# Reordering the swaps of x on the sync queue: block 0's ahead of block 2's loads, block 1's between the two loads of block 2

## Chip, core, metric

One core of one Trainium2 chip. The metric is the device time of one execution in microseconds (us). The kernel before takes 156.68 us (median of 3 runs, 156.55 to 157.26). Profiled spans are about 1.7 us shorter than the times, because the span runs from the first to the last instruction.

## The reference, cut to what matters

```python
g = sigmoid((x * gate_w).sum(-1, keepdims=True))        # x: 2048 x 448
q, k, v = split(x @ wqkv)                               # 16 heads of 28
phi_q = concat(softmax(q @ w_phi), softmax(-q @ w_phi)) # per head, phi_k likewise
o = (phi_q @ (phi_k^T v)) / (phi_q . sum(phi_k)) @ wo   # linear attention
b = gelu(x @ w1 + b1) @ w2 + b2
out = g * o + (1 - g) * b
```

The kernel works on x transposed (channels on partitions), in four blocks of 512 rows, numbered 0 to 3. 448 channels are seven chunks of 64. For much of the work PE runs two 64-row matmuls side by side, one on the upper and one on the lower half of the partitions, so each half needs all seven chunks of its own block of x. Half of these chunks lie on the wrong partitions, and copies inside SBUF, the "swaps", bring them across.

## The kernel before

Block 0 is turned by PE. Blocks 1 to 3 come by transposing DMAs, each as a wide one (384 channels) and a narrow one (the last 128). All of this and the swaps is issued from the sync queue (SP), in this order:

```python
def load_x(b):                                          # transposed load of block b
    blk = slice(b * 512, (b + 1) * 512)
    nc.sync.dma_start_transpose(xT[:, 0:3, blk], x[blk, 0:384])     # wide
    nc.sync.dma_start_transpose(xT[:, 3, blk], x[blk, 320:448])     # narrow
def swap_x(h):                                          # blocks 2h (even) and 2h+1 (odd)
    nc.sync.dma_start(xS[0:HP, :, h, :], xT[HP:P, :, ev])           # even
    nc.sync.dma_start(xS[HP:P, 0:3, h, :], xT[0:HP, 0:3, od])       # odd
...
load_wT(WkT, D); load_wT(WqT, 0); load_x(1)
... # weights are prepared; POOL copies the last chunk of block 1:
nc.gpsimd.dma_start(x1o, xT[HP:P, 3, 512:1024])
load_x(2)
swap_w(WqS, Wpq)        # query weights, two copies
swap_x(0)
load_x(3)
swap_w(WkS, Wpk)        # key weights
swap_x(1)
swap_w(WvS, WvG, 3)     # value weights
... # then w1, wo, w2
k_pair(0); k_pair(1); k_pair(2); k_pair(3); v_both()    # keys, values of blocks 0, 1
for g in range(4): q_pair(g, 0)                         # first use of swap_x(0)
for r in range(4): k_two(r); v_two(r); q_pair(r, 1)     # first use of swap_x(1), WvS
```

v_both uses x1o. After this part PE goes on with the feed-forward and the output without waiting.

The softmax here doesn't subtract the row's maximum and nothing guards it: scores larger than these inputs give would overflow.

## Time and profile before

| | before |
|---|---|
| time, median | 156.68 us |
| PE busy | 149.5 us, 97% of the span |
| PE's waits | 1.1 us at the start, 0.9 us for the odd swap of blocks 0 and 1 |
| odd swap of blocks 0 and 1: issue, landing | 16.40, 20.99 |
| odd swap of blocks 2 and 3: issue, landing | 22.71, 26.7 |

A DMA has two times: its issue, drawn on the queue SPq, and its landing, when the data are there. "x2" behind a line is a count. The lines of the profile are shown in the prediction.

### The profile page before, as it was taken

The page shows a single profiled execution, that of the slowest core. Times are in us where ns is not written, and L with a number is a line of the kernel's source. Part 1 is how long each engine was busy: PE and PEld are TensorE (multiplying, and loading weights), DVE is VectorE, ACT ScalarE, POOL GpSimd, SP SyncE. Part 2 cuts the span into 40 slices and gives each one's busy share as a digit, 9 for nine tenths or more (in the row PEclk, how much of TensorE's full clock was granted, in tenths as well). Part 3 has the DMA queues.
Part 4 walks back from the last instruction along what each step waited for, and adds up shares of the span by engine and source line. Part 5 has one row for each costly group of instructions (what it writes and reads, how often), then busy time and mean ns, then how long its engine had stood idle before and what let it go on. Part 6 is the DMA issues. An engine that isn't in the chain of part 4 may idle for free.

```text
span 154.7 us, 3189 instructions
## 1 busy us (share of the span) xinstructions
PE 149.5 (97%) x1302; PEld 81.2 (53%) x1302; DVE 83.1 (54%) x244; ACT 77.2 (50%) x93; POOL 34.1 (22%) x38
## 2 busy tenths in 40 slices
PE   7999979999999999999999999999999999999991
PEld 2775435555555854444444455555556555555561
DVE  3454989379892050000000059999977999977100
ACT  2569919999889626776767640111311111111121
POOL 7951596919876000000000000000000000000000
PEclk9999999999999999999999999999999999999999
DMA  4999999999993000000000001114332124338401
GB/s 150 229 232 154 209 233 254 221 222 215 218 356 130 4 0 4 0 0 4 0 0 0 4 0 34 34 38 96 92 96 64 40 64 92 82 82 39 121 31 30
DMA packets 28306, 14.98 MB, mean 97 GB/s; under 512 B 19938, under 2 KB 27876, under 8 KB 28292
## 3 DMA queue, kind: packets, MB, share of 16 engines
q1 hardware_dynamic: 27012, 14.00, 42.1%
q10 hardware_dynamic: 1152, 0.65, 1.5%
q0 software_dynamic: 128, 0.13, 0.7%
q8 instruction: 10, 0.16, 0.4%
q14 instruction: 4, 0.03, 0.1%
HBM read 6.11 MB, written 1.84 MB: 51 GB/s over the span
## 4 chain that ended last, share of the span: by engine, by line
PE 84%; SPq 9%; DMA 3%; issue 1%; DVE 0%; ACT 0%; ACTq 0%
PE hp L442 27%; PE y L501 27%; PE pq L320 8%; PE y L507 8%; PE nm L457 4%; PE v_ps L304 3%; PE pk L312 3%; DMA xS<-xT 3%; SPq L136 3%; PE acc L331 2%; SPq L132 2%; SPq L133 2%; SPq L384 1%; SPq L126 1%; SPq L141 0%
## 5 line engine op out<-in xcount | busy, mean ns | idle before, releaser
L501 PE MATMUL y<-w_sb,gel 128*128 128x448 bf16 (+2 forms) x238 | 45.2, 341 | 0.0
L442 PE MATMUL hp<-xT,w_sb 64*128 64x512 bf16 x196 | 42.3, 376 | 0.0
L442 PE MATMUL hp<-xS,w_sb 64*128 64x512 bf16 x196 | 41.9, 376 | 0.0
L447 ACT ACTIVATE gel<-hp,b1T 128x1024 bf16<-128x1024 f32 x28 | 30.8, 1110 | 13.0 <-PE hp L442 13.0
L510 ACT ACTIVATE res<-y,ungate 128x448 bf16<-128x448 f32 (+2 forms) x17 | 10.4, 611 | 50.3 <-PE y L507 50.2
L501 PEld LDWEIGHTS <-gel 128*128 128x128 bf16 x238 | 22.6, 98 | 19.6
L442 PEld LDWEIGHTS <-w_sb 64*128 64x128 bf16 x392 | 19.6, 94 | 22.5
L276 POOL TENSOR_TENSOR phik<-phik,rec 128x1792 bf16<-128x1792 bf16 (+1 forms) x8 | 24.9, 3126 | 9.8 <-DVE rec L273 9.8
L462 DVE COPY st<-nm 128x32 f32<-128x32 f32 x32 | 4.5, 184 | 35.5 <-PE nm L457 35.5
L478 DVE TENSOR_TENSOR tmp<-nm,al 128x448 bf16<-128x448 f32 x32 | 18.4, 617 | 0.0
L271 DVE TENSOR_REDUCE sums<-phik 128x64 f32<-128x1792 bf16 x8 | 16.0, 2000 | 2.8 <-ACT phik L264 2.8
L507 PE MATMUL y<-wo_sb,oT 128*128 128x448 bf16 (+2 forms) x68 | 14.7, 342 | 0.0
L320 PE MATMUL pq<-xT,Wpq 64*128 64x512 bf16 x56 | 13.0, 376 | 0.0
L320 PE MATMUL pq<-xS,WqS 64*128 64x512 bf16 x56 | 11.2, 376 | 0.9 <-DMA xS<-xT 0.9
L325 ACT ACTIVATE EqP<-pq 128x1024 bf16<-128x1024 f32 x8 | 8.4, 1051 | 5.1 <-PE pq L320 5.1
L193 DVE CAST vaug<-v_ps 128x896 bf16<-128x896 f32 x7 | 7.5, 1081 | 6.0 <-PE v_ps L304 3.3
L326 ACT ACTIVATE EqN<-pq 128x1024 bf16<-128x1024 f32 x8 | 8.4, 1055 | 0.0
L457 PE MATMUL nm<-KVbd,EqP 128*128 128x120 bf16 x64 | 8.3, 216 | 0.0
L457 PE MATMUL nm<-KVbd,EqN 128*128 128x120 bf16 x64 | 8.3, 216 | 0.0
L263 ACT ACTIVATE phik<-pk 128x896 bf16<-128x896 f32 x8 | 7.7, 961 | 0.3 <-PE pk L285 0.3
L507 PEld LDWEIGHTS <-oT 128*128 128x128 bf16 x68 | 6.0, 98 | 3.5
L264 ACT ACTIVATE phik<-pk 128x896 bf16<-128x896 f32 x8 | 7.8, 972 | 0.0
(99 smaller groups left out, 147.2 us busy)
## 6 DMA issues: line engine op xcount, KB each, us to landing
w_sb<-in_B_w_dram SPq DMA_DIRECT2D x4, 784.0 KB, 14.1
out_dram<-res SPq DMA_DIRECT2D x15, 112.0 KB, 1.9
w_sb<-in_B_w_dram SPq DMA_DIRECT2D x1, 1568.0 KB, 16.1
xS<-xT SPq DMA_DIRECT2D x2, 256.0 KB, 4.0
oT<-in_A_x_dram ACTq DMA_DIRECT2D x1, 448.0 KB, 3.2
xS<-xT SPq DMA_DIRECT2D x2, 192.0 KB, 4.3
WvS<-WvG SPq DMA_DIRECT2D x2, 168.4 KB, 3.9
wo_sb<-in_A_wo_dram SPq DMA_DIRECT2D x1, 336.0 KB, 17.1
```

What stands on the lines that cost most here:

```text
L271: nc.vector.reduce_sum(out=sums[:], in_=ph, axis=AX.X)
L276: eng.tensor_tensor(out=ph[:, lo:hi], in0=ph[:, lo:hi], in1=rec[:, lo:hi, :, None].to_broadcast([P, hi - lo, 2, DH]), op=ALU.mult)
L320: nc.tensor.matmul(pq[:, i, :], lhsT=w_half(Wpq, WqS, i, k)[:, g * P:(g + 1) * P], rhs=x_half(i, k, h), start=(k == 0), stop=(k == NK - 1))
L325: nc.scalar.activation(out=EqP[:, g, dst], in_=src, func=ACT.Exp)
L326: nc.scalar.activation(out=EqN[:, g, dst], in_=src, func=ACT.Exp, scale=-1.0)
L442: nc.tensor.matmul(hp[:, i, :], lhsT=w1_sb[i * HP:(i + 1) * HP, k, j * P:(j + 1) * P], rhs=x_half(i, k, h), start=(k == 0), stop=(k == NK ...
L447: nc.scalar.activation(out=gel[h][:, j, :], in_=hp[:].rearrange("p a b -> p (a b)"), func=ACT.Gelu_apprx_tanh, bias=b1T[:, j:j + 1])
L457: nc.tensor.matmul(nm[s][:, g * 2 * KW:(g + 1) * 2 * KW], lhsT=E[:, g, tok], rhs=KVbd[:, g, s, :], start=True, stop=True)
L478: nc.vector.tensor_tensor(out=tmp[:, s, :].rearrange("p (x h d) -> p x h d", x=NPR, h=2), in0=nmv[s][:, :, 0:PW].rearrange("p x (h d) -> p ...
L501: nc.tensor.matmul(y, lhsT=gel[t // 8][:, j, (t % 8) * P:(t % 8 + 1) * P], rhs=w2_sb[:, j, cols], start=(j == 0), stop=False)
L507: nc.tensor.matmul(y, lhsT=oT[:, c, tok], rhs=wo_sb[:, c, cols], start=False, stop=(c == NC4 - 1))
L510: nc.scalar.activation(out=res[:, cols], in_=y, func=ACT.Copy, scale=ungate[:, t:t + 1])
```

## The change

The intent: the odd swap is what PE waits for, so it is moved ahead of the narrow load of block 2, and the even swap, whose source is ready early, to the front.

```diff
-    load_x(2)
+    swap_x(0, "even")
+    load_x(2, "wide")
     swap_w(WqS, Wpq)
-    swap_x(0)
+    swap_x(0, "odd")
+    load_x(2, "rest")
     load_x(3)
```

load_x and swap_x get an argument that issues one of their two DMAs (cut here). Nothing else changes.

More of the change, by code (lines that the diff above doesn't have):

```diff
@@ L128, with load_x, swap_x @@
     nc.scalar.dma_start(wphi[:, 0:3, :], wphi_rows[0:384, :].rearrange("(c p) b -> p c b", p=P))
-    def load_x(b):
+    def load_x(b, part=None):
         blk = slice(b * 512, (b + 1) * 512)
-        nc.sync.dma_start_transpose(xT[:, 0:3, blk], x[blk, 0:384])
-        nc.sync.dma_start_transpose(xT[:, 3, blk], x[blk, 320:448])
+        if part != "rest":
+            nc.sync.dma_start_transpose(xT[:, 0:3, blk], x[blk, 0:384])
+        if part != "wide":
+            nc.sync.dma_start_transpose(xT[:, 3, blk], x[blk, 320:448])
     def load_wT(W, base):
         nc.sync.dma_start_transpose(W[:], A_wqkv[:, base:base + NC4 * P])
-    def swap_x(h):
+    def swap_x(h, part=None):
         ev = slice(2 * h * 512, 2 * h * 512 + 512)
         od = slice(2 * h * 512 + 512, 2 * h * 512 + 1024)
-        nc.sync.dma_start(xS[0:HP, :, h, :], xT[HP:P, :, ev])
-        nc.sync.dma_start(xS[HP:P, 0:3, h, :], xT[0:HP, 0:3, od])
+        if part != "odd":
+            nc.sync.dma_start(xS[0:HP, :, h, :], xT[HP:P, :, ev])
+        if part != "even":
+            nc.sync.dma_start(xS[HP:P, 0:3, h, :], xT[0:HP, 0:3, od])
     load_wT(WkT, D)
```

## The prediction

> **What bounds the kernel now.** I read the page first (busy shares and the chain that ended last), then PE's waits, then the timelines of PE and of the sync queue between 10 and 30 us, then the DMA's share in short windows. The page says that PE is the bound, and the list of PE's waits says how little of its time is not work:
>
> ```profile
> PE 149.5 (97%) x1302; PEld 81.2 (53%) x1302; DVE 83.1 (54%) x244; ACT 77.2 (50%) x93; POOL 34.1 (22%) x38
> PE 84%; SPq 9%; DMA 3%; issue 1%; DVE 0%; ACT 0%; ACTq 0%
> ...
> PE warm_ps L367 <- DVE w_sb L115: 1.1, 1, 1.1
> PE pq L320 <- DMA xS<-xT: 0.9, 1, 0.9
> ```
>
> The last two lines are all the waits of PE: 1.1 us at the very start, and one wait of 0.9 us, for a swapped copy of x. So the change can win at most this one hole. Behind it the chain is PE without a break to the end; ahead of it it is the sync queue, issuing DMAs one after the other:
>
> ```profile
> 10.27 1.71 SPq L132
> ...
> 12.03 1.26 SPq L133
> ...
> 13.47 0.56 SPq L383
> ...
> 14.08 1.52 SPq L384
> ...
> 16.40 4.59 DMA xS<-xT
> ```
>
> Columns are start, length, what. L132 and L133 are the wide and the narrow transposed load of x block 2, L383 and L384 the two swaps of the query weights; left out after them is L141, the even swap of x (source: block 0, issued at 15.64), and the last line is the odd swap (source: block 1), which lands at 16.40 + 4.59 = 20.99 us. PE's timeline shows what it holds up:
>
> ```profile
> 19.77 0.38 PE L320 MATMUL pq<-xT,Wpq 64*128 64x512 bf16 x1
> 21.03 0.39 PE L320 MATMUL pq<-xS,WqS 64*128 64x512 bf16 x2 [0.89 <-DMA xS<-xT]
> 21.24 0.39 PE L320 MATMUL pq<-xT,Wpq 64*128 64x512 bf16 x2
> ```
>
> The second matmul of the first query product (k = 0, lower half) is already one on the odd swap. Pairs start 0.21 us apart (21.03, 21.24), so without a wait it would have started at 19.77 + 0.21 = 19.98; it started at 21.03. The hole as it counts for the end is 21.03 - 19.98 = 1.05 us; the 0.89 is smaller because the matmul before is drawn to its modelled end.
>
> **What the skill says.** (1) The Trainium skill, "DMA: Bandwidth & Descriptors", section "Queues, rings and completion order": on each DMA engine descriptors are taken in ring order. The trace agrees as far as it goes: the copies that I could follow land in the order of issue (key swaps issued at 20.57 and 21.20 land 3.3 and 3.5 us later, the odd swap of blocks 2 and 3 from 22.71 after 4.0, the last value swap from 24.27 after 3.9). So moving an issue ahead of a transfer takes that transfer's time out of the landing. (2) "Perfetto Trace Analysis", section "DMA Instruction — HWDGE (DVE, Sync)": the issue's window is descriptor generation, not the data's movement. It agrees: 0.60 us of issue against 4.59 to landing. (3) "DMA: Bandwidth & Descriptors", section "Two DMAs through the same engine are not ordered": a copy that reads what an earlier DMA wrote has to wait for its completion. The odd swap reads block 1, loaded by DMA; the even one reads block 0, which came by PE transposes and DVE and ACT copies that end at 7.1 us. Neither wait binds: block 1's wide load, issued at 7.12, has 5.7 us to landing or less, so it is there by 12.8. (4) The same page, "Issuing engines are not separate DMA queues": the copy that POOL issues at 13.59 (x1o) shares the engines. The trace shows the collision below.
>
> **The change part by part.** Nothing is added or removed: the same DMAs, the same bytes, the same PE work. Only the order on the sync queue changes, to: even swap (block 0), wide load 2, query-weight swaps, odd swap, narrow load 2, load 3, and then as before.
>
> *The odd swap's issue.* The narrow load leaves the place ahead of it: 12.03 to 13.29, 1.26 us and a gap of 0.05. The even swap is ahead of it in both. So its issue moves from 16.40 to about 15.1. The query swaps would start at about 10.27 + 0.70 + 1.75 = 12.7; their source is complete then (last ACT cast of Wpq 11.45 + 0.91 = 12.36), so no wait is put in.
>
> *The odd swap's landing.* The DMA is loaded all through this stretch, so I count what stands in the ring ahead of it:
>
> ```profile
> 13.00:14.00 1.00, 1.00 (x7) 0.54 (x6) 0.00 (x0) 1.00 (x2) 0.41 (x1) 1.00 1.25 264
> 14.00:15.00 1.00, 1.00 (x7) 0.52 (x6) 0.63 (x1) 1.00 (x2) 0.11 (x1) 1.00 1.94 121
> 15.00:15.50 0.50, 0.50 (x5) 0.25 (x3) 0.50 (x1) 0.50 (x2) 0.00 (x0) 1.00 0.18 10
> 15.50:16.00 0.50, 0.50 (x4) 0.24 (x3) 0.50 (x1) 0.50 (x2) 0.00 (x0) 1.00 0.58 211
> ```
>
> The last two columns are the DMA share and GB/s. There is a hole: from 15.0 to about 15.9 hardly anything moves (0.18, 10 GB/s), though the query swaps were issued from 13.47 on. What still moves are a few 256 B packets, the tail of load 2, beside POOL's copy; the plain copies begin when that tail is through, at about 15.9. My reading, an inference from this one place: plain copies do not start before the transposed load ahead of them is finished on every engine, and POOL's copy delays that tail.
>
> After 15.9, before: query swaps 448 KB, even 256 KB and odd 192 KB, 896 KB (0.92 MB) at 205 to 224 GB/s, 4.3 us, so 20.3, and some 0.6 us to the recorded landing (the odd swap's last packet ends at 20.4 in the trace): 20.9, against 20.99 measured. After the change the even swap goes ahead: block 1's narrow load landed 4.3 us after its issue at 8.97, at 13.3, so its packets were through by 12.6; the even swap takes 0.26 MB / 0.21 = 1.25 us to 13.8, the wide load 0.39 MB at 285 GB/s 1.4 us to 15.2; with POOL's copy in it (it moves at 14 to 16 us whatever the sync queue does) I take 16.0. Then query swaps and odd swap, 640 KB = 0.66 MB at 0.21, 3.1 us: 19.1, landing at 19.7. That is 0.3 us before PE asks at 19.98. So the hole closes, by 1.05 us; if POOL's copy costs more than I take, some tenths of it stay.
>
> *What comes next.* If PE runs ahead by g from 20 us on, it asks g earlier for everything later. Two copies are close: the odd swap of blocks 2 and 3, landing at 22.71 + 4.0 = 26.7, is first used at 27.06, and the second value swap, landing at 24.27 + 3.9 = 28.17, at 28.39:
>
> ```profile
> 27.06 0.36 PE L312 MATMUL pk<-WkS,xS 64*128 64x448 bf16 x2
> ...
> 28.39 0.36 PE L304 MATMUL v_ps<-WvS,xS 64*128 64x449 bf16 x2
> ```
>
> If these landings stay, g is only 27.06 - 26.74 = 0.3 at the first and 28.39 - 28.21 = 0.2 at the second, and most of the 1.05 comes back as new waits 7 and 8 us later. They may come earlier: in the hole of 0.9 us the ring now has the even swap (1.25 us) done by 16.0 where before it had the narrow load (0.13 MB, 0.45 us), so everything behind is ahead by 1.25 - 0.45 = 0.8 us. But their issue is not: the same DMAs stand ahead of them, so it stays near 22.71 and 24.27. The quickest landings nearby are 3.3 and 3.5 us. With 3.3: 26.0 and 27.6, so g is up to 27.06 - 26.05 = 1.0 and 28.39 - 27.6 = 0.8. I take 0.75 as the middle. Later nothing is close: w1's first half, used at 43.55, has landed by about 35; ACT's idle time in the feed-forward is 13.0 us, POOL's last multiply ends at 48.9 and its data are read after 51.5.
>
> Sum: 156.68 - 0.75 = 155.93, say 155.9 us.
>
> **The rivals.** *A, the wait moves:* the later swaps land as before; 0.2 us are won, 156.5. For it: same bytes, same issue times. Against it: the hole in the DMA at 15 us, which the new order fills. *B, all is won:* 1.05, so 155.6; it needs the last value swap to land by 27.3, 3.1 us after its issue, quicker than any in this stretch, or a sync queue that also gains (the L384 issue of 1.52 us, against 0.59 for the key weights' like, may be a stall that goes). *C, a loss:* the new order changes between transposed loads and plain copies once more (a plain copy after load 1, another after the wide load 2). If each change costs a hole like that at 15 us, 0.9 us, the odd swap lands at about 20.6 and the later ones up to 0.9 late: up to 0.7 us at 28 us, 157.3. Against: at the change after load 3 (22.0 to 23.0, share 1.11) there is no such hole, and POOL's copy was absent there. Another loss, the narrow load 2 coming too late, is out: it is first read in the value and key products at 27 us and follows the odd swap at once.
>
> **Range and chances.** I give the middle case and B 65%, A 25%, C 10%. The three times of before spread over 0.7 us, so some tenths belong on both sides: 155.3 to 156.7. Two per cent is 3.1 us; the one wait is 1.05, so faster is all but impossible, and a loss of 3 us would need several new holes on PE. Faster 0.01, same 0.98, slower 0.01.
>
> **What would show it.** Right: PE's wait on xS at 20 to 21 us gone or under 0.2 us; odd swap issued near 15.1, landing near 19.7; the DMA's hole near 15 us smaller; key products starting near 25.9; PE's waits listing at most some tenths at 26 to 28 us, for xS or WvS. Wrong: a wait of more than 0.4 us at 26 to 28 us (A); a DMA hole at 12 to 13 us as well, or the first query product no earlier than 21 us (C); a changed wait elsewhere, of POOL's copy above all, whose product PE reads at 19.4 us.

## The result

The changed kernel takes 157.19 us (median of 6 runs, 156.91 to 157.71), before 156.67 in the same rounds. Executions over 1.5% slower than the fastest of the same kernel are left out of the means. Ratios here are the mean time of one kernel's runs over that of the other's runs of the same rounds, so they are not quite the ratio of the medians: 1.0028, with a 95% interval of 1.0004 to 1.0053. In later rounds on another occasion (after2) it was 1.0012 (0.9996 to 1.0028). So it is slower by 0.1 to 0.3%, some 0.2 to 0.4 us, though the second interval just includes 1. The prediction's 155.9 with a range of 155.3 to 156.7 was wrong.

The page of the changed kernel, its busy shares and its chain:

```profile
PE 150.2 (96%) x1302; PEld 83.3 (54%) x1302; DVE 83.1 (53%) x244; ACT 77.3 (50%) x93; POOL 34.0 (22%) x38
...
PE 86%; SPq 8%; DMA 2%; ACT 1%; issue 1%; DVE 0%; ACTq 0%
```

All of PE's waits in it (on whom, total us, times, longest us):

```profile
PE warm_ps L371 <- DVE w_sb L115: 1.1, 1, 1.1
PE pk L316 <- DMA xS<-xT: 0.6, 1, 0.6
PE v_ps L222 <- DMA oT<-xT: 0.5, 1, 0.5
```

The wait on the query product (pq) is gone from the list. Two others stand in its place: one in the key product of blocks 2 and 3 (pk), for their swap, and one for POOL's copy of the last chunk of block 1 (x1o, which lives in the tile oT). PE's timeline has where:

```profile
20.39 0.36 PE L222 MATMUL v_ps<-WvS,oT 64*128 64x449 bf16 x1 [0.53 <-DMA oT<-xT]
...
21.09 0.39 PE L324 MATMUL pq<-xS,WqS 64*128 64x512 bf16 x2
...
27.93 0.36 PE L316 MATMUL pk<-WkS,xS 64*128 64x448 bf16 x2 [0.65 <-DMA xS<-xT]
```

In this profile the pq wait is hidden rather than won. The odd swap of blocks 0 and 1 landed at 21.04, 6.49 us after its issue (the packed trace has the landing; the views print none for it), and the matmul that reads it starts at 21.09. Without the 0.53 us for x1o just ahead, PE would have come to it some 0.5 us sooner and waited. In the second profile, after2, it landed 4.92 us after its issue, and PE did not wait.

The sync queue of the changed kernel (start, length of the issue, line, what; L144 even swap, L146 odd swap, L133 wide load, L135 narrow load):

```profile
14.55 0.72 SPq L146 DMA_DIRECT2D xS<-xT  x1
15.32 1.88 SPq L135 DMA_TRANSPOSE xT<-in_A_x_dram  x1
17.24 3.37 SPq L133 DMA_TRANSPOSE xT<-in_A_x_dram  x1
20.66 1.26 SPq L135 DMA_TRANSPOSE xT<-in_A_x_dram  x1
...
24.01 0.62 SPq L146 DMA_DIRECT2D xS<-xT  x1
```

The odd swap of blocks 0 and 1 is issued 1.85 us earlier than before (14.55 against 16.40). But the narrow load 2 and the wide load 3 behind it take 1.88 and 3.37 us to issue, and the odd swap of blocks 2 and 3 comes at 24.01, where it was at 22.71. The DMA in the same windows as those that the prediction shows (the last two columns are the DMA share and GB/s):

```profile
14.00:15.00 1.00, 1.00 (x7) 0.54 (x6) 0.21 (x1) 1.00 (x2) 0.52 (x1) 1.00 1.34 197
15.00:15.50 0.50, 0.50 (x5) 0.23 (x4) 0.50 (x1) 0.50 (x2) 0.00 (x0) 1.00 4.21 97
15.50:16.00 0.50, 0.50 (x4) 0.28 (x3) 0.50 (x1) 0.50 (x2) 0.00 (x0) 1.00 0.03 3
16.00:17.00 1.00, 1.00 (x8) 0.49 (x6) 0.97 (x2) 1.00 (x2) 0.00 (x0) 1.00 0.54 116
```

The hole is still there: 3 GB/s from 15.5 to 16.0, and most of the next window too. A share above 1 ahead of it means packets that were started and then hung. This time the wide load 2 hangs in it, not the tail of the narrow one.

**A measure free of the start.** From profile to profile the key products start anywhere from 10.7 to 11.7 us, in the same program too (before: 10.88 and 11.33). So I count from the first key matmul (0) and compare: the start of the first swapped query matmul, the issue of the odd swap of blocks 2 and 3, the first key matmul that uses it, and the first feed-forward matmul, after which PE never waits. All are starts in the timelines, subtracted; the ratios are those of each kernel to before in its own rounds.

The two profiles of the changed kernel lie 0.73 us apart in the last stretch (33.31 and 32.58), those of the other kernels profiled twice 0.00 to 0.12. So a difference of some tenths between two single profiles shows nothing by itself.

| kernel | query | odd swap 2/3 issued | its first use | feed-forward | ratio to before |
|---|---|---|---|---|---|
| before | 10.15 | 11.83 | 16.18 | 32.67 | |
| before2 | 10.15 | 11.84 | 16.19 | 32.68 | 1.0003 (0.9988 to 1.0018) |
| changed | 9.81 | 12.73 | 16.65 | 33.31 | 1.0028 (1.0004 to 1.0053) |
| changed again (after2) | 9.00 | 11.90 | 15.86 | 32.58 | 1.0012 (0.9996 to 1.0028) |
| only_even | 10.32 | 12.46 | 16.36 | 33.01 | 1.0003 (0.9984 to 1.0022) |
| only_rest | 9.92 | 12.82 | 16.75 | 33.45 | 1.0013 (0.9990 to 1.0036) |
| before_nox1o | 9.40 | 11.08 | 15.44 | 32.01 | 0.9986 (0.9966 to 1.0006) |
| after_nox1o | 9.40 | 12.31 | 16.30 | 32.99 | 1.0000 (0.9981 to 1.0018) |
| grouped | 8.87 | 12.61 | 16.55 | 33.21 | 1.0037 (1.0014 to 1.0061) |
| after_early | 8.87 | 11.50 | 15.69 | 32.43 | 0.9999 (0.9976 to 1.0023) |
| after_early2 | 8.87 | 11.71 | 15.82 | 32.55 | 1.0003 (0.9986 to 1.0019) |
| before_late | 10.44 | 12.11 | 16.47 | 32.96 | 1.0033 (1.0012 to 1.0053) |
| after_late | 9.01 | 11.90 | 15.89 | 32.60 | 1.0030 (1.0009 to 1.0052) |
| early_act | 8.91 | 13.42 | 16.24 | 32.98 | 1.0033 (1.0010 to 1.0057) |
| after_merge | 9.12 | 12.04 | 16.00 | 32.76 | 0.9984 (0.9963 to 1.0006) |
| early_merge | 8.91 | 11.41 | 15.38 | 32.14 | 0.9962 (0.9943 to 0.9982) |
| early_merge2 | 8.87 | 11.35 | 15.37 | 32.14 | 0.9982 (0.9968 to 0.9996) |
| only_rest_merge | 8.87 | 11.01 | 15.14 | 31.83 | 0.9985 (0.9957 to 1.0013) |
| rest_merge_late | 9.70 | 11.84 | 15.83 | 32.53 | 1.0008 (0.9995 to 1.0021) |

Two things stand in it. Where PE waits on the odd swap of blocks 2 and 3, its first use comes 3.9 to 4.2 us after its issue, in all kernels but early_act. And the feed-forward follows that first use by 16.5 to 16.8 us in every one. The landings say the same: in all kernels of the table but before, before2, before_nox1o and before_late, this first use starts within 0.1 us of the landing of that swap, also where the list of waits names none. So what counts is when this swap is issued and lands. In the kernel before the use (16.18) was still set by the query product, but 11.83 + 4.0 = 15.83 was only 0.35 us behind it.

### The profile page after: what moved, and what is told of

Its sections match the earlier page's. It is cut to its first block, busy times and chain, and to the rows that moved or that the text cites. A ratio compares the mean times of both kernels' runs of the same rounds, so it can differ in the third digit from the quotient of the medians.

```text
span 155.7 us, 3191 instructions
## 1 busy us (share of the span) xinstructions
PE 150.2 (96%) x1302; PEld 83.3 (54%) x1302; DVE 83.1 (53%) x244; ACT 77.3 (50%) x93; POOL 34.0 (22%) x38
## 4 chain that ended last, share of the span: by engine, by line
PE 86%; SPq 8%; DMA 2%; ACT 1%; issue 1%; DVE 0%; ACTq 0%
PE hp L448 27%; PE y L507 27%; PE y L513 8%; PE nm L463 4%; PE pq L324 4%; PE v_ps L308 4%; PE pk L316 4%; SPq L133 3%; DMA xS<-xT 2%; PE acc L335 2%; PE v_ps L209 2%; PE warm_ps L371 2%; SPq L135 2%; PE xp L354 1%; SPq L388 1%; SPq L387 1%
## 5 line engine op out<-in xcount | busy, mean ns | idle before, releaser
L507 PEld LDWEIGHTS <-gel 128*128 128x128 bf16 x238 | 22.6, 98 | 19.7
L448 PEld LDWEIGHTS <-w_sb 64*128 64x128 bf16 x392 | 20.5, 94 | 21.6
L513 PE MATMUL y<-wo_sb,oT 128*128 128x448 bf16 (+2 forms) x68 | 14.7, 341 | 0.0
L324 PE MATMUL pq<-xT,Wpq 64*128 64x512 bf16 x56 | 13.2, 376 | 0.0
## 6 DMA issues: line engine op xcount, KB each, us to landing
w_sb<-in_B_w_dram SPq DMA_DIRECT2D x4, 784.0 KB, 14.1
w_sb<-in_B_w_dram SPq DMA_DIRECT2D x1, 1568.0 KB, 16.5
wo_sb<-in_A_wo_dram SPq DMA_DIRECT2D x1, 336.0 KB, 16.8
```

What stands on the lines that cost most here:

```text
L324: nc.tensor.matmul(pq[:, i, :], lhsT=w_half(Wpq, WqS, i, k)[:, g * P:(g + 1) * P], rhs=x_half(i, k, h), start=(k == 0), stop=(k == NK - 1))
L448: nc.tensor.matmul(hp[:, i, :], lhsT=w1_sb[i * HP:(i + 1) * HP, k, j * P:(j + 1) * P], rhs=x_half(i, k, h), start=(k == 0), stop=(k == NK ...
L507: nc.tensor.matmul(y, lhsT=gel[t // 8][:, j, (t % 8) * P:(t % 8 + 1) * P], rhs=w2_sb[:, j, cols], start=(j == 0), stop=False)
L513: nc.tensor.matmul(y, lhsT=oT[:, c, tok], rhs=wo_sb[:, c, cols], start=False, stop=(c == NC4 - 1))
```

## The experiments

Ratio, times and traces are from rounds with the kernel before on the same chip; times below are medians.

**The parts of the change by themselves.** only_even and only_rest:

```diff
 # only_even                         # only_rest
+swap_x(0, "even")                    load_x(2, "wide")
 load_x(2)                            swap_w(WqS, Wpq)
 swap_w(WqS, Wpq)                     swap_x(0)
+swap_x(0, "odd")                    +load_x(2, "rest")
 load_x(3)                            load_x(3)
```

> Only the first half of the change: the even swap ahead of block 2's loads, both loads of block 2 in one piece. Theory 1 (each plain copy put between transposed loads costs DMA time, so everything behind lands later): the odd swap lands after 21 us and PE waits on it about 1 us as before or more; time 156.7 to 157.3. Theory 2 (the loss comes from POOL's small copy x1o, which queues behind the query swaps when it is issued after them): here the query swaps are issued later than in the changed kernel, so x1o goes ahead of them, PE does not wait on it, and the time is that of before, 156.7, or a little less. Theory 3 (the narrow load 2 placed behind the odd swap chokes the issue of load 3 and starves the DMA at 22 to 24 us): the wide load of block 3 is issued in about 1.9 us instead of 3.4 and the key product has no wait.

> Only the second half: wide load 2, query swaps, even, odd, then the narrow load 2. Theory 1: one more change between loads and copies, so the later swaps land later than before; 156.7 to 157.2. Theory 2: x1o is issued after the query swaps (which go 1.3 us earlier than before), so PE waits on it some 0.5 us; but the odd swap lands about 0.5 us earlier. Theory 3: wide load 3 takes over 3 us to issue, and a wait of 0.5 us or more in the key product at 27 to 28 us.

Measured: only_even 157.01 against 157.04 us, PE waiting 1.1 us on the odd swap. only_rest 157.06, with 0.7 us on the odd swap at 21 us and 0.6 us in the key product. Neither part wins, and in both the odd swap of blocks 2 and 3 is issued later (12.46 and 12.82 against 11.83). The wide load 3 takes 2.23 and 2.69 us to issue, between 1.85 of before and 3.37. Both still have the stop. Theory 2's order was borne out in only_even: x1o, issued by POOL at 14.25, moved from 17.3 to 17.5, just ahead of the query swaps, and PE did not wait for it. Theory 1's expectations fit both runs too, so these two do not decide between the theories.

**Without POOL's copy.** Both kernels with full 128-row matmuls for the values of block 1 in place of x1o:

```diff
-for c in range(3): ...     # 12 full matmuls, then 4 half ones with x1o
+for c in range(NC4): ...   # 16 full ones
-nc.gpsimd.dma_start(x1o, xT[HP:P, 3, 512:1024])
```

> The kernel before without POOL's copy x1o: the value product of block 1 is made with full 128-row matmuls (16 instead of 12 and 4 half ones, about 0.4 us more on PE). No hold by x1o is possible. Before waited on the odd swap till 21.0 us anyway, so the added PE work hides in that wait: all theories 156.3 to 156.8, and if x1o delayed the tail of load 2 and so the odd swap, up to 0.6 us less.

> The changed kernel without x1o, full matmuls instead (0.4 us more PE work). Theory 2 (x1o is the cause): PE is not held at 19.8 us and the time falls to or below the same of before without x1o. Theories 1 and 3 (the later swaps land late whatever x1o does): the wait in the key product near 27 us stays or grows by what is won at 20 us, and the time stays above that of before without x1o by 0.3 us or more.

Measured: 156.81 and 157.08 us against 157.04. In after_nox1o PE is not held at 20 us, but waits 0.7 us in the key product. So POOL's copy does not look like the cause of the loss: without it the changed order is still 0.27 us slower, just short of the 0.3 us asked for and barely beyond the spread of the six times. Its hold of 0.5 us in the first profile of the changed kernel did not come back in the second, after2. And the hole in the DMA is there in both, without x1o: what I had laid to POOL's copy was not its doing.

One thing was not followed up. In before_nox1o PE does not wait on the odd swap at all, and in spite of the added PE work its stretch to the feed-forward (32.01) is the second shortest of the table. Its interval (0.9966 to 1.0006) reaches 1, and it was not run again, so whether dropping this copy is by itself the better change stays open.

**What stops the DMA.** I listed the packets in these traces. Each of the long stops ends a fixed time after one other packet: one of 16 KB on the queue that the page calls "instruction". The page of the kernel before has ten such packets:

```profile
q8 instruction: 10, 0.16, 0.4%
```

The Trainium skill, "Perfetto Trace Analysis", section "The 4-stage abstract model", says that instructions are 64 bytes; so 16 KB are 256 of them, and ten times 256 is 2560, about the 2604 instructions that the page counts for PE (1302 matmuls and 1302 weight loads). I infer that they are PE's instructions being fetched. A count supports it: in all 20 kept traces the first of these packets starts when PE has started 177 to 199 of its instructions, and the last six follow each other about 256 PE instructions apart (246 to 268 in the two profiles of before). By the packets (a stop: under 60 GB/s for 0.4 us or more beside the fetch; the last column was worked out before rounding):

| trace | fetch | stop | from fetch's end to stop's end |
|---|---|---|---|
| before | 13.7 to 14.9 | 14.9 to 15.7 | 0.7 |
| before2 | 14.2 to 15.4 | 14.7 to 16.1 | 0.7 |
| changed | 14.6 to 15.9 | 15.2 to 16.6 | 0.7 |
| changed again (after2) | 13.9 to 14.9 | 14.4 to 15.6 | 0.7 |
| only_even | 13.9 to 15.2 | 14.5 to 16.0 | 0.8 |
| only_rest | 14.4 to 15.4 | 14.8 to 16.1 | 0.7 |
| before_nox1o | 14.1 to 15.1 | 15.0 to 15.8 | 0.7 |
| after_nox1o | 13.7 to 15.0 | 14.3 to 15.7 | 0.7 |
| before_late | 14.1 to 15.3 | 14.6 to 16.0 | 0.7 |
| after_late | 14.5 to 15.4 | 14.8 to 16.2 | 0.8 |
| after_merge | 13.2 to 14.3 | 13.7 to 15.1 | 0.8 |
| early_merge | 13.1 to 14.4 | 13.9 to 15.1 | 0.7 |
| rest_merge_late | 13.7 to 14.6 | 13.9 to 15.4 | 0.7 |
| grouped | 13.8 to 14.7 | none (nothing to move from 13.8 to 14.2) | |
| after_early | 12.1 to 13.2 | none | |
| after_early2 | 11.9 to 13.1 | none | |
| early_act | 12.0 to 13.3 | none | |
| early_merge2 | 11.4 to 12.7 | none | |
| only_rest_merge | 13.9 to 15.0 | none | |

In the traces with a stop, packets of a transposed load are in flight when it begins. Where hardly anything but plain copies is, there is none (the first or last packets of a transposed load overlap an end of the fetch there by at most 0.3 us, in only_rest_merge); and at 35 us, when the next fetch meets the plain load of w1, the kernel before keeps moving over 200 GB/s. Not every pause needs a fetch, though: transposed loads also fall under 60 GB/s for about 0.5 us with no such packet beside them, in before2 from 12.7 to 13.2, in after_early2 from 14.0 to 14.5, in early_merge2 from 13.6 to 14.1. What makes these was not looked into. "No stop" below means none beside the fetch.

To test it, grouped puts plain copies where the fetch falls, after_early moves the fetch ahead, into the even swap, and before_late and after_late were to move it behind load 2:

```diff
 # grouped                  # after_early: narrow warm-up, 22 PE instructions more
 swap_x(0, "even")         -dummies(7)      # each 512 columns
 swap_w(WqS, Wpq)          +dummies(18)     # each 192 columns
 swap_x(0, "odd")           # before_late, after_late: float32 warm-up
 load_x(2)                 -dummies(7)
 load_x(3)                 +dummies(2)      # float32, 512 columns
```

> Even swap, query swaps, odd swap, and only then loads 2 and 3 in one piece. Theory 4 (new, from the traces so far: when PE's instruction fetch of 16 KB, at 14 to 16 us, meets a transposed load in flight, all transfers stop until some 0.75 us after the fetch ends): here only plain copies are in flight at 14 to 16 us, so there is no stop; the odd swap lands by 18 us, nothing waits on it, the swaps of blocks 2 and 3 land no later than before, and the time is 155.6 to 156.3. Theory 1 (changes between loads and copies cost): as few changes as in the kernel before, so also faster, but the stop of 0.8 us or more at 14 to 16 us stays. Theory 3 (load 3's issue chokes when it stands right behind load 2): both loads stand together here, so wide load 3 takes over 3 us to issue and the key product waits 0.5 us or more.

> The changed kernel with 18 narrow warm-up matmuls in place of 7 wide ones: 22 more PE instructions in the same time, so PE's instruction fetch comes some 2 us earlier, about 12.3 to 13.7, when the even swap, a plain copy, is in flight. Theory 4: the full stop of 1.4 us at 15.5 goes or shrinks to the tail of load 1 (under 0.6 us), later swaps land about 1 us earlier, and the time falls to 156.0 to 156.6. Theories 1 and 3: fetch does not matter, a stop stays at 15 to 17 us, time as the changed kernel's, 157.0 to 157.3.

> The kernel before with 2 float32 warm-up matmuls in place of 7 bf16 ones, about the same PE time and 13 PE instructions fewer, so the fetch comes 1.2 us later, about 15.3, when loads 2 are nearly or quite through. Theory 4: no stop or under 0.4 us, the odd swap lands 0.5 us or more earlier, PE's wait on it under 0.4 us, time 156.0 to 156.6. If the fetch does not matter: PE waits 0.9 us as before, 156.6 to 157.1.

> The changed kernel with the same 2 warm-up matmuls: fetch at 15.8 to 16.3, behind the wide load 2, with the query swaps in flight. Theory 4: no stop, the odd swap lands by 19.6, later swaps 1 us earlier than in the changed kernel, time 155.8 to 156.5, at least as fast as before_late. Theories 1 and 3: as the changed kernel, 157.0 to 157.3.

after_early is nearly as theory 4 has it: 156.65 us against 156.70 (156.0 to 156.6 expected), the fetch at 12.1, no stop, the first query product without a wait (8.87). Its repeat has the same, in these windows:

```profile
14.00:15.00 1.00, 1.00 (x7) 0.52 (x6) 0.44 (x1) 1.00 (x2) 0.02 (x1) 1.00 0.69 146
15.00:16.00 1.00, 1.00 (x7) 0.49 (x5) 1.00 (x1) 1.00 (x2) 0.00 (x0) 1.00 1.26 325
```

grouped has next to nothing in flight when its fetch begins: the even swap has just ended. The plain query swaps start to move at 14.3, while the fetch still runs. It has no wait on the query product; yet it is the slowest, 157.37, over 1 us above what theory 4 said, because of the key product:

```profile
28.03 0.36 PE L316 MATMUL pk<-WkS,xS 64*128 64x448 bf16 x2 [1.29 <-DMA xS<-xT]
```

Its query swaps wait for their weights until 13.11, so the queue stands idle ahead of them, and all four transposed loads are then issued in a row, from 16.11 to 21.99, with the DMA at times under 90 GB/s at 20 to 21 us: I take the issue to be the limit there. The odd swap of blocks 2 and 3 is issued at 12.61. before_late and after_late missed their aim: the fetch came at 14.1 and 14.5, hardly later, and met load 2. One reason is in the page: it counts 1299 matmuls and 1299 weight loads, only 6 PE instructions fewer and not 13, for each float32 warm-up matmul stands as two. They were slower (157.22 and 157.24), and before_late decides nothing on the stop.

**The changed kernel, the moved fetch and its control, side by side.**

> The changed kernel once more, as the partner of the other three on the same chip. All theories: 156.9 to 157.4, ratio to before 1.001 to 1.005. Theory 4: its trace again has a full stop of the DMA of over 1 us that ends 0.7 to 0.8 us after PE's instruction fetch ends.

> The changed kernel with the 18 narrow warm-up matmuls once more. Theory 4: 0.3 to 0.7 us less than the changed kernel beside it, no full stop in the trace. If the earlier gain was chance: the same time within 0.2 us.

> Control: the same 18 narrow warm-up matmuls in the kernel before, where transposed loads are in flight without a break from 4 to 15 us. Theory 4: the stop moves with the fetch, to about 12.5 to 14, and hits load 2 or the tail of load 1 in the middle; the time is that of before or up to 0.6 us more (156.7 to 157.4). If the gain of after_early came from the warm-up itself and not from where the fetch falls: this one is 0.4 us or more faster than before.

after2 156.83 (just under what was expected), after_early2 156.62 and before_early 156.59 us against 156.62. So moving the fetch is worth about 0.2 us to the changed kernel here, less than the 0.3 to 0.7 expected and within the spread of the times (0.5 between the first measurements, which were rounds on different occasions), and the same warm-up gains nothing in the kernel before (1.0004, interval 0.9986 to 1.0023), as expected. That profile of before_early fell into a slow execution (177.02 us at a clock of 0.855), so I take nothing from it.

But even without the stop the changed kernel only draws level with before. PE waits 0.43 and 0.56 us in the key product: the odd swap of blocks 2 and 3 is issued at 11.50 and 11.71, hardly sooner than the 11.83 of before.

**Taking issue time off the queue.** First by giving the key weights' swaps to ACT's queue, on top of after_early:

```diff
-swap_w(WkS, Wpk)                         # on the sync queue
+nc.scalar.dma_start(WkS[0:HP, ...], Wpk[HP:P, ...])   # both, behind k_pair(3)
```

> The changed kernel with the narrow warm-up matmuls, and the two swaps of the key weights issued from ACT's queue, after its last activation of the first key products, while it is idle. That takes 1.2 us of issue out of the sync queue ahead of the swaps of blocks 2 and 3. If the rest of PE's wait at 27 us (0.4 us in after_early) is the sync queue's issue time, the wait goes and the time is 156.1 to 156.4; if it is the DMA's throughput, the wait stays and the time is after_early's, 156.5 to 156.8.

It went the other way, 157.28 us (a slow execution of 159.12 left out). The sync queue stands still ahead of the odd swap:

```profile
19.82 1.34 SPq L135 DMA_TRANSPOSE xT<-in_A_x_dram  x1
21.27 0.62 SPq L144 DMA_DIRECT2D xS<-xT  x1
24.89 0.59 SPq L146 DMA_DIRECT2D xS<-xT  x1
```

The list of the queue's waits says 2.9 us for a load of x: the odd swap reads the wide load 3, which landed only then. The ACT copies, issued at 17.86 and 18.99, were in the DMA at the same time as that load. The issue was free, but the data that it needs came later. That answers neither of the two expectations.

Then by merging the two narrow loads into one:

```diff
-load_x(2, "rest")
-load_x(3)
+nc.sync.dma_start_transpose(xT[:, 3, 1024:2048], x[1024:2048, 320:448])
+load_x(3, "wide")
```

> The kernel before against itself: a second profile and the noise of the method. Ratio 0.998 to 1.002. Its trace again has the stop at 15 to 16 us ending 0.75 us after the fetch, and PE's only long wait is on the odd swap at 20 to 21.5 us, 0.6 to 1.3 us.

> The changed kernel with the narrow loads of blocks 2 and 3 made one transposed load of 1024 columns, where the narrow load 2 stood. Two issues of 1.3 to 1.9 us become one of about 1.6. If issue time on the sync queue is what makes the swaps of blocks 2 and 3 late, the odd one is issued 0.7 to 1 us earlier than in the changed kernel and PE's wait at 27 us falls below 0.2 us: time 156.2 to 156.7. If it is the DMA's throughput, the same bytes take as long, the wait of 0.6 us stays: 156.8 to 157.2.

> The same merged load, and the 18 narrow warm-up matmuls that put PE's instruction fetch beside the even swap. With issue time as the cause: no stop, no wait on the odd swap, no wait at 27 us; PE runs through from 11 us on, and the time is 155.7 to 156.2, faster than the kernel before by 0.4 us or more. With throughput as the cause: 156.4 to 156.7.

> Even swap left at its old place (after the query swaps), narrow loads merged behind the odd swap. If the even swap's early place matters, the odd swap lands later here and PE waits on it 0.4 us or more, 156.5 to 157.0; if not, the time is that of after_merge.

before2, the kernel before against itself, is at 1.0003 (156.53 against 156.52 us), its two profiles agree to 0.01 us in the table, and its one long wait of PE is again the odd swap:

```profile
21.48 0.39 PE L320 MATMUL pq<-xS,WqS 64*128 64x512 bf16 x2 [0.88 <-DMA xS<-xT]
```

after_merge took 156.25 us against 156.52, early_merge 155.92, only_rest_merge 156.38. In only_rest_merge the even swap is at its old place and PE still has no wait on the odd one, so its early place was not needed there. early_merge is faster than before with an interval clear of 1. In its profile the odd swap of blocks 2 and 3 is issued at 11.41. It kept a stop in that profile, since its fetch came later (13.1) than in the other kernels with the narrow warm-up, when PE had started 199 instructions; why so late, I don't know. after_merge still waits 0.69 us in the key product, which its expectation had going if issue time was the cause: its odd swap is issued only at 12.04, after the landing of the wide load 3, for which the queue waits 0.7 us.

**The best ones again.**

> The best kernel once more: 155.6 to 156.2, ratio to before 0.994 to 0.998. In its trace no wait of PE above 0.3 us between 11 and 43 us.

> only_rest_merge with 2 float32 warm-up matmuls of 384 columns in place of 7 bf16 ones of 512 (13 PE instructions fewer), so PE's instruction fetch starts 0.5 to 1 us later, about 14.7 to 15.4, when the wide load 2 is through and the query swaps are in flight. If the slow ones of only_rest_merge's times are those in which the fetch met the load's tail, all times here are in the fast group, 155.4 to 156.0, and the trace has no stop at 14 to 17 us. If not, the times spread as before, 155.5 to 157.1.

early_merge2: 156.26 us against 156.57, ratio 0.9982 (0.9968 to 0.9996). All of PE's waits in its profile:

```profile
PE warm_ps L371 <- DVE w_sb L115: 1.1, 1, 1.1
PE v_ps L209 <- DVE xT L197: 0.2, 1, 0.2
```

And its sync queue (L399 is the merged load):

```profile
15.58 2.04 SPq L399 DMA_TRANSPOSE xT<-in_A_x_dram  x1
17.66 1.55 SPq L133 DMA_TRANSPOSE xT<-in_A_x_dram  x1
...
22.06 0.62 SPq L146 DMA_DIRECT2D xS<-xT  x1
```

No stop, no wait on a swap in the list, and the odd swap at 22.06. By the starts a little is still lost: that swap landed at 26.04, and its first matmul starts at 26.08, 0.46 us after the matmul before it, where such pairs otherwise stand 0.2 apart. And the queue waits 0.6 us for the wide load 3 before it issues this swap, so here it is that load, not the time to issue, that holds it. Its median is 0.06 us outside what I expected, but its interval again lies below 1: this version beats both kernels, by 0.2 to 0.4%. rest_merge_late failed to delay the fetch (13.7), had a stop from 13.9 to 15.4, and took 156.68. So whether the two groups in only_rest_merge's times (155.55, 155.57; 156.19 to 157.08) are the fetch missing or meeting load 2 stays open. Its profiled run was one of the fast ones and has no stop; the stretch up to the feed-forward, 31.83, is the shortest of all.

## Why the prediction was wrong

*Right.* PE's only loss to win was the one wait of 1.05 us. The odd swap's issue was foreseen at 15.1 and came at 14.55. The places where a gain could be lost again, the key product's swap at 27 us above all, were named with their slack of 0.3 us, and so was x1o. Counted from the first key matmul, the odd swap of blocks 0 and 1 was to land at 19.7 - 10.88 = 8.8; it landed at 8.96 in after2, but at 9.76 in the first profile (10.11 before).

*The step that failed: "everything behind is ahead by 1.25 - 0.45 = 0.8 us", and with it a landing 3.3 us after issue.* From it the prediction let g, PE's lead, rise to 1.0. In both profiles of the changed kernel the odd swap of blocks 2 and 3 landed 3.9 us after its issue, where it had been 4.0, and in all kernels but early_act 3.9 to 4.2 us passed to its first use wherever PE waited, also where the DMA had no stop. Nor was it issued ahead: at 12.73 and 11.90 from the first key matmul, against 11.83 and 11.84. So nothing of the 0.8 us arrived.

*The reading behind it.* The prediction took the hole at 15 us for a matter of load 2's tail and POOL's copy, which the even swap would fill. before_nox1o shows the hole without POOL's copy. It goes with the fetch and hits whatever transposed load is in flight: in the first profile of the changed kernel the wide load 2 hung in it, and ended at 17.2, not at 16.0. One reading was off as well: the odd swap's last packet ends at 20.1 in the trace, not at 20.4, so 0.9 us and not 0.6 passed to its landing, and 19.7 should have been 20.0, with no margin left.

*What took its place: rival A.* With the issue and the landing of that swap unmoved, at most 16.18 - 15.83 = 0.35 us could be won. after2 won 0.10 of it up to the feed-forward (32.58 against 32.68); the first profile lost 0.64 (33.31), as the wide load 3 took 3.37 us to issue. The mean of the two, 32.95, is 0.27 us over before, which is about what the times say. Where the 3.37 comes from I can only argue: it stands behind a DMA held up by the stop and behind a narrow load that used to be ahead, and in after_early2, without the stop, the same issue took 1.50. That the 3.37 needs both was not tested; nor was why one profile had it and the other had 2.06. Rival C's 157.3 came nearest to the measured 157.19, but by luck: its cause, the changes between loads and copies, is not what the runs show.

*The range.* All three rivals were there, A even with its 0.2 us; the chances went to the middle case because the hole was believed to be understood from one place in one trace. That was called an inference in the text and then used as a quantity twice.

*Theories 1 and 3 of the experiments.* grouped, with as few changes between loads and copies as before, was the slowest, and the hole in the changed kernel stands inside the wide load 2 and not at such a change: theory 1 is not needed, though no run shuts it out. Theory 3 holds in so far as fewer issues ahead of the later swaps bring them sooner: with the narrow warm-up, merging two loads brought the first use of the odd swap from 15.69 and 15.82 to 15.38 and 15.37. In the changed kernel itself the wait stayed (after_merge).

## What to carry to other kernels

When a wait on a queue's transfer is moved away, look at once at the next transfer of the same queue: if its slack is smaller than the wait, that slack is all there is to win, unless the next transfer itself comes sooner; here merging two loads brought it forward. A hole in the DMA that ends a fixed time after some other packet is better explained by listing the packets than by what was issued nearby. Compare stretches inside the trace rather than whole spans when the start wanders more than the effect is worth.

## What the Trainium skill lacked or had wrong

- No page has it that an instruction fetch can stop transposed loads. "DMA: Bandwidth & Descriptors", section "Rules for kernel authors", says "A transpose next to ordinary DMAs needs nothing". That is about correctness, and results were correct here; but for time it lacks this: in 13 of the 19 traces tabled, a 16 KB fetch of 1.0 to 1.3 us with a transposed load in flight brought the data transfers to a stop (under 60 GB/s) for 0.7 to 1.5 us, until 0.7 to 0.8 us after the fetch ended. Beside plain transfers there was no stop. That the fetch is PE's is inferred, from the counts of PE instructions and from 22 added ones moving it some 2 us in four of the five fast traces that have them (in early_merge it came at 13.1). The point would belong to "Runtime: NRT & Kernel Launch", section "Instruction fetch mechanics", as well.
- The same page, section "Issuing engines are not separate DMA queues", calls the issue "usually small relative to the DMA itself". For narrow transposed loads it is not: 1.26 us of issue on the sync queue for 0.13 MB, which the DMA moves in about 0.45 us at 290 GB/s (an estimate), and with two of them merged into one the key product's wait went from 0.56 us (after_early2) to none in the list (early_merge2).
- No page gives how far the issue of a transposed load can stretch: the wide load 3, the same bytes each time, took 1.50 to 3.37 us to issue. What stretches it was not shown.
